# Transfers given out two at a time and a new order of work in a fused normalisation, state-space convolution and feed-forward kernel

## The chip, the core and the metric

The kernel runs on one core of one Trainium2 chip. A core has a matrix engine (TensorE, PE in the profile; its weight loads are PEld), a vector engine (VectorE, DVE), a scalar engine (ScalarE, ACT), a general engine (GpSimd, POOL), a sync engine (SyncE, SP) that here only gives out transfers, and 16 DMA engines that carry them. Data is worked on in SBUF, a memory of 128 partitions; PE writes its results into PSUM banks. Each engine runs its own list of instructions strictly in order and waits on semaphores for the others. The metric is device time in microseconds, the median of the timed runs.

## The reference

The input is one sequence of 2048 rows of 512 features. A condition vector gives six modulation vectors. The first half is a normalisation, a long convolution with a kernel built from 128 complex exponentials per feature, and a gated addition; the second half is a normalisation, a feed-forward part with squared ReLU, and a gated addition.

```python
def ssm(u, A_re, A_im, B_re, B_im, C_re, C_im, log_dt, Dskip):
    dt = jnp.exp(log_dt)[:, None]
    logdA = dt * (A_re + 1j * A_im)
    P = jnp.exp(logdA[:, :, None] * jnp.arange(L)[None, None, :])
    K = jnp.einsum("dn,dnl,dn->dl", Cc, P, dt * Bc).real
    # y = causal convolution of u with K along the sequence, through an FFT of length 2L
    return y + u * Dskip

def ffn(x, w1, b1, w2, b2):
    h = jnp.einsum("bsd,df->bsf", x, w1) + b1
    r = jnp.where(h > 0, h, 0)
    return jnp.einsum("bsf,fd->bsd", r * r, w2) + b2

sa, ca, ga, sb, cb, gb = split(silu(c) @ w_mod)
x = x + ga * ssm(layernorm(x) * (1 + ca) + sa, ...)
x = x + gb * ffn(layernorm(x) * (1 + cb) + sb, ...)
```

## The kernel before

The first half. The 2048 rows come in as 16 blocks of 128 rows by 512 features (`xt`, into tiles named `xy`). DVE takes their statistics (`bn_stats`, L595, L596), POOL makes the reciprocal deviation, and for every block `row_pieces` subtracts the mean and multiplies by the modulation (DVE, L657), scales a selection matrix (ACT, L659), multiplies by it on PE, which also adds the shift (L661, L664), and copies the result to the tile `big` (ACT, L667). PE has three banks named `ps` for this and for what follows, and one named `kg`.

The parameters of the convolution are worked out in two groups of four chunks of 64 features (`parameters`, L511 to L577): eight products on POOL (L526 to L533), roundings and absolute values on ACT (L535 to L545), an arctangent and a sine on ACT (L552, L561), shifts on DVE and integer additions on POOL (L564 to L574). `kgen_exp` fills tables with exponentials on ACT (L786).

The convolution runs on eight chunks of 64 features as a transform in two stages on PE, with constants that are loaded: `stage1` (L701, copied by ACT in L703) and `stage2` (L711, copied in L735). The input's spectrum goes through `u_pieces`; the kernel's 32 units are generated by POOL, ACT and DVE (`kgen_...`, L795 to L832), summed by PE into `kg` (L839) and transformed by `finish`. Products of the two spectra are taken on DVE (L849), which needs the input's spectrum twice: as it is, and with its two halves of 64 partitions exchanged. `swap_piece` makes the exchanged copy with two transfers from SBUF to SBUF, one for each half. PE sums the products (L857), DVE copies them (L863), and an inverse transform (L1024, with the constant `i2c`) gives the rows back.

The second half splits w1, w2 and the activations into a high and a low part of a faster number format (L973, L974, L977, L996) and computes 56 steps of two matmul groups (L1115 to L1118 and L1149 to L1151), three products each.

The order of the work. The program is first recorded in the order of the code; `ORDER` says, for each of the 32 kernel units, which pieces of the other work are recorded after it (r a row block, A to H an input chunk, 0 to 7 a swap, a to h a product chunk, x a table of exponentials, l the late modulation, w a load of a part of w1). Then `keep_order` puts every engine's instructions into one fixed list: it walks through the program with estimated durations, and at each step gives an engine, of the work that is ready, the one with the longest path to the end. `HURRY` adds or takes off urgency, in nanoseconds, for some kinds of work. The walk also has a model of how PE's instructions are fetched in packets, behind transfers. SP's list keeps the order of the recorded program. All loads, swaps and stores that matter here are given out by SP, one after the other: parameters and rows (L447 to L466), constants and modulation weights, swaps (L742), w1 (L933), `i2c` (L965), rows again for the gated addition (L984, L1040), w2 (L1084), stores (L1159). The list `behind` of pairs that `keep_order` takes is empty before.

Of the kernel before, what the change touches and what calls it, by code (L numbers as in the profile page):

```python
# [44 lines left out]
ORDER = (  # L45
    "rrrrrrrrrrrrrrrrCABCBCBlCBCBACBBA.AA.CAABA.xx.0Caaaa.a.aD1aa..bDbbbEE.DD.bDD2bEb.b.cDDEcccc.cxcc"
    "F3..EF.EEdddd.FFEd.GF4Fd.d.deGeeFeG.GGFx.HH.G.5HeeeeffGffGfww.6H..Hff.fH.gHHgggw.g.w7.hwghwhghgw"
    "w"
).split(".")
# [56 lines left out]


def weight(ins):

    out = ins.outs[0] if ins.outs and hasattr(ins.outs[0], "bass_ap") else None  # L110
    n = free_size(out) if out is not None else 1
    if "DMA" in type(ins).__name__:
        inside = not any("Dram" in type(a.bass_ap.tensor).__name__.title() for a in (*ins.ins, *ins.outs))
        return 60, n * out.ap[0][1] * 4 / (180 if inside else 360)
    match str(ins.engine).split(".")[-1]:
# [16 lines left out]
            if n == 1:  # L132
                t = 200
# [17 lines left out]
            t = 30  # L151
# [12 lines left out]
def keep_order(tc, traced, slots, in_turn, whole, urgent, behind):  # L164
# [107 lines left out]
    for _ in groups:  # L272
# [7 lines left out]
        if e == "PE":  # L280
# [55 lines left out]
def tile_adaln_ssm_ffn(  # L336
# [244 lines left out]

    urgent, behind = {}, []

# [154 lines left out]
    def swap_piece(c):  # L738
        xs, sw = xus[c], spectrum()
        sws[c] = sw  # L740
        for h in range(2):
            nc.sync.dma_start(sw[64 * h : 64 * h + 64], xs[64 - 64 * h : 128 - 64 * h])  # L742
        yield
# [184 lines left out]
    def load_pieces():  # L928
        for f, n in W1_PARTS:
            h = f // 896  # L930
            if f == 896 * h:
                raw1.append(held(kp, f"k0{h}", f"raw1{h}", [P, 4, 896]))
            nc.sync.dma_start(raw1[h][:, :, f - 896 * h : f - 896 * h + n], w1v[:, :, f : f + n])  # L933
            yield
# [29 lines left out]
    nc.gpsimd.tensor_copy(i2c[:, 0, 0, 0:1], runs(sws[NC - 1])[:, 0:1])  # L964
    nc.sync.dma_start(i2c, c_i2.rearrange("p (j r a) -> p j r a", j=64, r=2))  # L965

# [16 lines left out]
    for s in range(8):  # L983
        nc.sync.dma_start(xts[s], xt[s])  # L984
    w1la = held(ka, slots[na], "w1la", [P, 4, 512], FR)
# [30 lines left out]
    def inverse(s0, n):  # L1016
# [19 lines left out]
        for s in range(s0, s0 + n):  # L1036
            if s > 3:
                nc.gpsimd.tensor_add(x2[:, s], x2[:, s], d4(xts[s]))
                if s + 4 < 16:
                    nc.sync.dma_start(xts[s + 4], xt[s + 4])  # L1040

# [38 lines left out]
    def w2_split(t, n):  # L1080
        for i in range(n):
            wst = wsts[len(w2s) % 2]
            hi_, lo_ = t[:, 1024 * i : 1024 * i + 512], t[:, 1024 * i + 512 : 1024 * i + 1024]
            nc.sync.dma_start(wst, w2v[:, len(w2s)])  # L1084
            split(hi_, lo_, wst)
# [161 lines left out]
```

## Time and profile before

| | |
|---|---|
| runs | 639.13 us median of 3 (637.85 to 642.98) |
| the profiled execution | 637.81 us; span from the first to the last instruction 636.0 us |
| mean granted clock of PE | 0.99 |
| the first half | about 0 to 310 us |
| the steps of the feed-forward part | about 310 to 636 us |

A row of the profile names line, engine, operation, output and input tile and count; what stands in brackets is the time that the engine stood idle just before, and what ended it. "issue" there is a wait that nothing in the profile explains but the engine's own instruction supply. The page's slices show the course of the run: each digit is the busy share in a fortieth of the span, in tenths.

```profile
PE   1697897999999999898989999999999999999995
...
ACT  5957899889987948362856432253323433222220
POOL 6499699999999987039958100010000100000000
...
DMA  8942014022132403662333000100001000010001
```

### The profile page before, as it was taken

The numbers are of one execution on the slowest core, as the hardware profiler recorded it, in microseconds if no ns is written. First come the engines' busy times: TensorE is split into PE (matmuls) and PEld (weight loads), VectorE is DVE, ScalarE is ACT, GpSimd is POOL, SyncE is SP. The second block draws the span as 40 slices with busy tenths as digits, with TensorE's granted clock in tenths as the row PEclk, the third lists the DMA queues.
The fourth block names the chain that finished last, engine by engine and source line by source line (L and its number), as shares of the span: only waits on it lengthen the run. The fifth ranks groups of instructions, "written<-read, shape, count | busy, mean of one in ns | idle before, by whom it ended". The sixth has DMA issues, their size and how long they took to land.

```text
span 636.0 us, 21183 instructions
## 1 busy us (share of the span) xinstructions
PE 590.5 (93%) x9474; PEld 510.4 (80%) x9474; DVE 371.0 (58%) x652; ACT 349.6 (55%) x651; POOL 297.4 (47%) x247
## 2 busy tenths in 40 slices
PE   1697897999999999898989999999999999999995
PEld 1476797999998899897868888888888888888884
DVE  6886978899799688546655332533325332252223
ACT  5957899889987948362856432253323433222220
POOL 6499699999999987039958100010000100000000
PEclk9999999999999999899999999999999999999999
DMA  8942014022132403662333000100001000010001
GB/s 319 392 140 68 3 35 105 19 55 45 29 70 69 120 4 86 185 250 88 95 110 99 1 1 0 67 0 2 0 1 66 1 1 0 1 66 1 0 1 66
DMA packets 21707, 42.33 MB, mean 67 GB/s; under 512 B 3696, under 2 KB 9200, under 8 KB 20336
## 3 DMA queue, kind: packets, MB, share of 16 engines
q1 hardware_dynamic: 21184, 40.84, 21.0%
q8 instruction: 74, 1.21, 0.8%
q10 hardware_dynamic: 432, 0.14, 0.1%
q14 instruction: 17, 0.14, 0.1%
HBM read 28.39 MB, written 4.19 MB: 51 GB/s over the span
## 4 chain that ended last, share of the span: by engine, by line
PE 72%; ACT 9%; POOL 7%; DVE 5%; issue 4%; DMA 2%; DVEq 0%; SPq 0%; ACTq 0%; POOLq 0%
PE tg L1149 8%; PE tg L1151 8%; PE tg L1150 8%; PE ps L711 7%; PE ps L1115 6%; PE ps L701 6%; PE ps L1116 6%; PE ps L1118 6%; PE ps L857 6%; PE kg L839 3%; PE kg L1115 2%; PE kg L1116 2%; PE kg L1118 2%; PE tg L1024 1%; ACT xy L703 1%
## 5 line engine op out<-in xcount | busy, mean ns | idle before, releaser
L1135 ACT ACTIVATE xy<-ps,b1c 128x512 f32<-128x512 f32 x42 | 29.0, 690 | 126.2 <-PE ps L1118 126.2
L1137 DVE SCALAR_TENSOR_TENSOR ps<-ps,b1c,xy 128x512 f32<-128x512 f32 x42 | 31.8, 758 | 111.1 <-ACT xy L1135 111.1
L1060 POOL TENSOR_TENSOR big<-big,lo 128x512 f32<-128x512 f32 x12 | 15.7, 1306 | 151.8 <-DVE xy L1057 151.8
L711 PE MATMUL ps<-xy,t_sb 128*64 128x64 f32 x2048 | 67.4, 223 | 3.7 <-issue 2.5
L711 PEld LDWEIGHTS ps<-xy,t_sb 128*64 128x64 f32 x2048 | 63.9, 138 | 6.3 <-issue 3.0
L857 PE MATMUL ps<-e_sb,xy 128*64 128x128 f32 (+2 forms) x1152 | 64.2, 270 | 1.9 <-ACT xy L703 1.0
L857 PEld LDWEIGHTS ps<-e_sb,xy 128*64 128x64 f32 x1152 | 59.9, 142 | 3.6 <-ACT xy L703 1.4
L819 POOL TENSOR_TENSOR rtl<-tables 128x1024 f32<-128x1024 f32 x22 | 43.4, 1972 | 0.1
L703 ACT COPY xy<-ps 128x512 f32<-128x512 f32 x64 | 37.0, 598 | 7.7 <-PE ps L701 7.4
L849 DVE TENSOR_TENSOR xy<-ps,xy 128x512 f32<-128x512 f32 x64 | 39.9, 682 | 1.3 <-PE ps L711 1.1
L1115 PE MATMUL ps<-h0h,w1h 128*128 128x512 f32 (+1 forms) x96 | 36.0, 381 | 0.0
L795 POOL TENSOR_TENSOR rtl<-lo,big 128x1024 int32<-128x1024 int32 x16 | 34.3, 2145 | 3.1 <-ACT tg L807 2.5
L701 PE MATMUL ps<-d_sb,big 128*64 128x128 f32 x512 | 32.7, 275 | 2.9 <-ACT big L667 1.4
L701 PE MATMUL ps<-d_sb,ksb 128*64 128x128 f32 x512 | 34.3, 279 | 0.5 <-ACT xy L703 0.4
L863 DVE COPY big<-ps 128x256 f32<-128x256 f32 (+1 forms) x66 | 24.2, 407 | 18.0 <-PE ps L857 17.8
L795 POOL TENSOR_TENSOR llph<-lo,big 128x1024 int32<-128x1024 int32 x16 | 34.5, 2159 | 0.2 <-ACT tg L807 0.2
L701 PEld LDWEIGHTS ps<-d_sb,big 128*64 128x64 f32 x512 | 28.1, 137 | 4.3 <-ACT big L667 1.7
L1115 PE MATMUL ps<-h,w1h 128*128 128x512 f32 x80 | 31.4, 393 | 0.0
L1135 ACT ACTIVATE xy<-kg,b1c 128x512 f32<-128x512 f32 x14 | 9.7, 690 | 39.5 <-PE kg L1118 39.5
L1137 DVE SCALAR_TENSOR_TENSOR kg<-kg,b1c,xy 128x512 f32<-128x512 f32 x14 | 10.6, 756 | 34.0 <-ACT xy L1135 34.0
L701 PEld LDWEIGHTS ps<-d_sb,ksb 128*64 128x64 f32 x512 | 28.8, 140 | 1.6 <-ACT xy L703 0.7
L839 PE MATMUL kg<-rtl 128*32 128x64 f32 x1408 | 25.5, 221 | 4.3 <-issue 3.1
(287 smaller groups left out, 1606.7 us busy)
## 6 DMA issues: line engine op xcount, KB each, us to landing
xy<-xt SPq DMA_DIRECT2D x32, 256.0 KB, 5.5
xy<-xy SPq DMA_DIRECT2D x16, 512.0 KB, 6.0
xy<-w_mod SPq DMA_DIRECT2D x6, 1024.0 KB, 9.2
out_dram<-xy SPq DMA_DIRECT2D x16, 256.0 KB, 2.1
xy<-w SPq DMA_DIRECT2D x14, 256.0 KB, 2.7
raw<-w SPq DMA_DIRECT2D x6, 512.0 KB, 5.3
t_sb<-c_t SPq DMA_DIRECT2D x1, 2048.0 KB, 10.9
i2c<-c_i SPq DMA_DIRECT2D x1, 2048.0 KB, 9.9
```

What stands on the lines that cost most here:

```text
L701: nc.tensor.matmul(ps[64 * r : 64 * r + 64, 128 * i : 128 * i + 128], src[:, i], d1_sb[:, r], start=True, stop=True)
L711: nc.tensor.matmul(ps[64 * r : 64 * r + 64, 64 * i : 64 * i + 64].rearrange("p (h q t) -> p q h t", h=2, t=2), t2_sb[:, 8 * g + i, r], src ...
L795: nc.gpsimd.tensor_tensor(ph.rearrange("p d r (a b) -> p (d r) a b", a=4), bc(low_phase[:, us].rearrange("p d r b -> p (d r) b"), 2, 4), b ...
L819: nc.gpsimd.tensor_mul(am[:, 0, :, 32:96].rearrange("p d (v x) -> p d v x", v=2), bc(et[:, 256 + 8 * d0 : 384 + 8 * d0].rearrange("p (y a) ...
L839: nc.tensor.matmul(kps[32 * q : 32 * q + 32, d, :], am[:, r, 4 * q + d, 64:96], am[:, r, 4 * q + d, 0:64], start=(r == 0), stop=(r == 1))
L857: nc.tensor.matmul(ps[64 * m : 64 * m + 64], pairs(y)[:, g, i // 2, 64 * m : 64 * m + 64, i % 2], e1_sb[:, h].rearrange("p (r j) -> p r j" ...
L1115: pe.append(nc.tensor.matmul(ps, w1h[:, q, fs], hh[:, q, cols], start=(q == 0), stop=False))
L1116: pe.append(nc.tensor.matmul(ps, wl[:, q], hh[:, q, cols], start=False, stop=False))
L1118: pe.append(nc.tensor.matmul(ps, w1h[:, q, fs], hl[:, q, cols], start=False, stop=(q == 3)))
L1149: pe.append(nc.tensor.matmul(acc, r2l[:, ms], hi_, start=(t == 0), stop=False))
L1150: pe.append(nc.tensor.matmul(acc, r2h[:, ms], lo_, start=False, stop=False))
L1151: pe.append(nc.tensor.matmul(acc, r2h[:, ms], hi_, start=False, stop=(t == NF - 1)))
```

## The change

It has four parts. A helper `paced_load` issues a transfer on SP and, from the third one on, makes it wait until the transfer two places earlier in the same series has landed. The swaps, the loads of w1, `i2c`, the rows `xt` for the gated addition and w2 go through it; the first loads, the modulation weights and the stores don't. A swap's two halves are each cut in two along the free dimension, so that it is four transfers, and `i2c` is loaded in four pieces. The planner's constants for instruction packets and for the time that transfers occupy the queue are others. `ORDER` and `HURRY` are others.

```diff
+PACED = 2
-HURRY = (176674, 61960, 2605, 274089, 54201, -67055, -175605, 69371)
+HURRY = (147316, 134417, 27026, 378229, -185473, -185396, -357712, -713)
...
 ORDER = (
-    "rrrrrrrrrrrrrrrrCABCBCBlCBCBACBBA.AA.CAABA.xx.0Caaaa.a.aD1aa..bDbbbEE.DD.bDD2bEb.b.cDDEcccc.cxcc"
+    "rrrrrrrxrrxrrrrrrrCABCBCBCBCAACB.BBCBAAAAlAC...0aaaa1..aDaaa..DbbbbEE.D2D.DEbbD.xbDDb.EccccccE.F"
...
+    wait = mybir.DependencyInfo(mybir.DependencyClass.Sync, mybir.DependencyReason.DATA)
     for x, y in behind:
-        before[group[x]].add(group[y])
+        before[group[y.name]].add(group[x.name])
+        tc.add_manual_dep(y, x.name, wait, reason="pace")
...
-                    fetched = max(asked[0] + asked[1], min(behind_ns - 1800, asked[0] + 4300)) + 2350
-                asked = (max(t, fetched), 1100 if fetched > t else 600)
+                    fetched = max(asked[0] + asked[1], min(behind_ns, asked[0] + 4500)) + 2400
+                asked = (max(t, fetched), 1100 if fetched > t else 750)
...
-            queued.append((now, landed))
+            queued.append((now, landed + (-1000 if within(groups[g][0]) else -300)))
...
+    def paced_load(to, of):
+        ins = nc.sync.dma_start(to, of).ins
+        if len(paced) >= PACED:
+            behind.append((paced[-PACED], ins))
+        paced.append(ins)
...
         for h in range(2):
-            nc.sync.dma_start(sw[64 * h : 64 * h + 64], xs[64 - 64 * h : 128 - 64 * h])
+            for o in range(0, 2048, 1024):
+                paced_load(
+                    runs(sw)[64 * h : 64 * h + 64, o : o + 1024], runs(xs)[64 - 64 * h : 128 - 64 * h, o : o + 1024])
...
-    nc.sync.dma_start(i2c, c_i2.rearrange("p (j r a) -> p j r a", j=64, r=2))
+    for j in range(0, 64, 16):
+        paced_load(i2c[:, j : j + 16], c_i2.rearrange("p (j r a) -> p j r a", j=64, r=2)[:, j : j + 16])
```

The lines after the change are some 6 to 16 higher than before; all paced transfers carry line 591. How the change moves instructions is shown at two places. The first is SP's list at the end of the first half. Before (`raw` is w1 as loaded, `xy<-xy` the last swap):

```order
L933 DMA raw_4458<-w 128x4x256 x2
L933 DMA raw_4458<-w 128x4x128
L933 DMA raw_4458<-w 128x4x256
L742 DMA xy_97<-xy_94 64x2048 x2
L984 DMA xy_96<-xt 128x512 x2
L965 DMA i2c<-c_i 128x4096
L984 DMA xy_95<-xt 128x512 x4
```

SP's list at the same place after the change:

```order
L591 DMA raw_4391<-w 128x4x256 x2
L591 DMA xy_97<-xy_95 64x1024 x4
L591 DMA raw_4391<-w 128x4x128
L591 DMA raw_4391<-w 128x4x256
L591 DMA i2c<-c_i 128x1024 x4
L591 DMA xy_93<-xt 128x512 x4
```

The swap, now of four transfers, stands ahead of the last two loads of w1, and `i2c`, now of four, ahead of all rows `xt`.

The second place is the passage of the 16 row blocks, on DVE and on ACT. DVE's list before, at the third group of four blocks (`xy_91` holds the first four blocks, `xy_93` the third four, `xy_94` the last four; `st` and `mv` are statistics):

```order
L595 BN_STATS st_72<-xy_93 128x6
L595 BN_STATS st_73<-xy_93 128x6
L657 SCALAR_TENSOR_TENSOR xy_91<-xy_91,mv_71,kg_362 128x512 x3
L640 TENSOR_TENSOR s_360<-ps_157,gs_358 128x128
L595 BN_STATS st_74<-xy_93 128x6
L595 BN_STATS st_75<-xy_93 128x6
```

DVE's list after the change, where the first subtraction (now L670) stands:

```order
L575 TENSOR_SCALAR big_83<-big_83 128x4x64
L608 BN_STATS st_74<-xy_94 128x6
L608 BN_STATS st_75<-xy_94 128x6
L609 BN_AGGR mv_71<-st_73 128x2
L609 BN_AGGR mv_71<-st_74 128x2
L609 BN_AGGR mv_71<-st_75 128x2
L531 SCALAR_TENSOR_TENSOR big_83<-big_83 128x4x64
L670 SCALAR_TENSOR_TENSOR xy_91<-xy_91,mv_71,kg_362 128x512 x3
```

The first three subtractions moved from between the statistics of the third four blocks to behind those of the last four and behind the shifts of the first parameter group.

ACT's list before, from the fifth copy of a row block on (`big_84` takes the copied blocks, `big_83` holds the parameters, `ident` makes the selection matrix):

```order
L667 COPY big_84<-ps_159 128x128x4
L659 ACTIVATE big_83<-ident,mv_71 128x2x64
L667 COPY big_84<-ps_157 128x128x4
L659 ACTIVATE big_83<-ident,mv_71 128x2x64
L667 COPY big_84<-ps_158 128x128x4
```

ACT's list after the change, from the fifth copy on:

```order
L680 COPY big_84<-ps_159 128x128x4
L672 ACTIVATE big_83<-ident,mv_71 128x2x64
L541 ACTIVATE big_83<-big_83,magic 128x4x64
L542 ACTIVATE big_83<-big_83,magic 128x4x64
L550 ACTIVATE big_83<-big_83 128x4x64
L551 ACTIVATE big_83<-big_83 128x4x64
L543 ACTIVATE big_83<-big_83,unmagic 128x4x64
L680 COPY big_84<-ps_157 128x128x4
```

Five operations of the second parameter group (L535 to L545 before, L541 to L551 now) moved in ahead of the sixth copy; before, they stood behind the thirteenth and the fourteenth.

More of the change, by code (lines that the diff above doesn't have):

```diff
@@ L42 @@
 ON_DVE = {}
-HURRY = (176674, 61960, 2605, 274089, 54201, -67055, -175605, 69371)
+PACED = 2
+HURRY = (147316, 134417, 27026, 378229, -185473, -185396, -357712, -713)
 EXPS = [(0, 1), (1, 1), (2, 2), (4, 2), (6, 2)]
 ORDER = (
-    "rrrrrrrrrrrrrrrrCABCBCBlCBCBACBBA.AA.CAABA.xx.0Caaaa.a.aD1aa..bDbbbEE.DD.bDD2bEb.b.cDDEcccc.cxcc"
-    "F3..EF.EEdddd.FFEd.GF4Fd.d.deGeeFeG.GGFx.HH.G.5HeeeeffGffGfww.6H..Hff.fH.gHHgggw.g.w7.hwghwhghgw"
-    "w"
+    "rrrrrrrxrrxrrrrrrrCABCBCBCBCAACB.BBCBAAAAlAC...0aaaa1..aDaaa..DbbbbEE.D2D.DEbbD.xbDDb.EccccccE.F"
+    ".EEc3c.F.dddd.EdddFF4.dGFF..eGGeeeF.xGG.GeFHHe5Ge..effffGHf.wHf..HH.6ffwwwHg.g.gH.gww7g.gwgwhhhh"
+    "g"
 ).split(".")
@@ L105, in function_table, with within @@
     return {"Exp": 1, "Sin": 2, "Arctan": 3, "Sqrt": 4}.get(str(getattr(ins, "func", "")).split(".")[-1])
+def within(ins):
+    return not any("Dram" in type(a.bass_ap.tensor).__name__.title() for a in (*ins.ins, *ins.outs))
 def weight(ins):
@@ L112, in weight @@
     if "DMA" in type(ins).__name__:
-        inside = not any("Dram" in type(a.bass_ap.tensor).__name__.title() for a in (*ins.ins, *ins.outs))
-        return 60, n * out.ap[0][1] * 4 / (180 if inside else 360)
+        return 60, n * out.ap[0][1] * 4 / (180 if within(ins) else 360)
     match str(ins.engine).split(".")[-1]:
@@ L580, in parameters @@
         yield
-    urgent, behind = {}, []
+    urgent, behind, paced = {}, [], []
+    def paced_load(to, of):
[3 more added lines that the diff above has]
+        paced.append(ins)
     def hurry(start, ns):
@@ L932, in load_pieces @@
                 raw1.append(held(kp, f"k0{h}", f"raw1{h}", [P, 4, 896]))
-            nc.sync.dma_start(raw1[h][:, :, f - 896 * h : f - 896 * h + n], w1v[:, :, f : f + n])
+            paced_load(raw1[h][:, :, f - 896 * h : f - 896 * h + n], w1v[:, :, f : f + n])
             yield
@@ L983, in tile_adaln_ssm_ffn @@
     for s in range(8):
-        nc.sync.dma_start(xts[s], xt[s])
+        paced_load(xts[s], xt[s])
     w1la = held(ka, slots[na], "w1la", [P, 4, 512], FR)
@@ L1039, in inverse @@
                 if s + 4 < 16:
-                    nc.sync.dma_start(xts[s + 4], xt[s + 4])
+                    paced_load(xts[s + 4], xt[s + 4])
     def statistics(s):
@@ L1083, in w2_split @@
             hi_, lo_ = t[:, 1024 * i : 1024 * i + 512], t[:, 1024 * i + 512 : 1024 * i + 1024]
-            nc.sync.dma_start(wst, w2v[:, len(w2s)])
+            paced_load(wst, w2v[:, len(w2s)])
             split(hi_, lo_, wst)
```

## The prediction

> **What bounds the kernel now.** I read the page's first part, then its slices, the windows, what PE waited for, and the timelines of the places where PE stood still. The first two rows give busy time by engine, share and instructions; the third is one long window (busy us and count of PE, PEld, DVE, ACT, POOL, then granted clock, DMA share, GB/s); the fourth is a window of the second half.
>
> ```profile
> span 636.0 us, 21183 instructions
> PE 590.5 (93%) x9474; PEld 510.4 (80%) x9474; DVE 371.0 (58%) x652; ACT 349.6 (55%) x651; POOL 297.4 (47%) x247
> ...
> 85.00:345.00 260.00, 246.80 (x6922) 227.89 (x6918) 199.71 (x361) 193.63 (x327) 216.66 (x156) 0.99 0.32 87
> ...
> 360.00:380.00 20.00, 20.00 (x91) 16.53 (x90) 7.47 (x11) 8.40 (x15) 1.62 (x2) 1.00 0.00 0
> ```
>
> PE is the bound. From about 330 us it computes the two matmuls of the feed-forward part without a gap, on an order that the change keeps; nothing can be won there. PE is idle for 636.0 - 590.5 = 45.5 us: 260.0 - 246.8 = 13.2 us of it between 85 and 345, most of the rest ahead of 85, where data is not there yet. So the change is worth what it does to PE's gaps and to PE's clock. What PE waited for (total us, times, longest):
>
> ```profile
> PE kg L839 <- issue: 3.1, 3, 2.3
> ...
> PE ps L711 <- issue: 2.5, 4, 1.4
> ...
> PE tg L1024 <- issue: 1.8, 2, 1.1
> ...
> PE ps L1064 <- issue: 1.4, 1, 1.4
> ```
>
> These four make 3.1 + 2.5 + 1.8 + 1.4 = 8.8 us in which no other engine held PE: it waited for its own instructions. The timelines show why, twice:
>
> ```profile
> 92.16 14.78 SPq L742 DMA_DIRECT2D xy<-xy  x4
> ...
> 96.37 1.85 PE L711 MATMUL ps<-xy,t_sb 128*64 128x64 f32 x56 [0.48 <-ACT xy L703]
> ...
> 99.66 1.39 PE L711 MATMUL ps<-xy,t_sb 128*64 128x64 f32 x40 [1.43 <-issue]
> ...
> 254.89 2.99 SPq L933 DMA_DIRECT2D raw<-w  x4
> ...
> 261.47 0.64 PE L839 MATMUL kg<-rtl 128*32 128x64 f32 x26
> ...
> 262.83 1.11 SPq L742 DMA_DIRECT2D xy<-xy  x2
> ...
> 264.39 0.92 PE L839 MATMUL kg<-rtl 128*32 128x64 f32 x38 [2.28 <-issue]
> ```
>
> A group of 64 matmuls that needs nothing new breaks after 26, once with four loads of weights in flight, and one of L711 breaks with a swap in flight. Queue 8 brings the instructions of PE (packets, MB, share of the engines):
>
> ```profile
> q8 instruction: 74, 1.21, 0.8%
> ```
>
> 74 packets for PE's 9474 matmuls and 9474 weight loads are 256 instructions each, 128 pairs: PE stops where a packet ends and the next has not come, because it queues behind large transfers. The gap of 2.28 us has a second price, the clock:
>
> ```profile
> 260.00:265.00 5.00, 2.72 (x117) 2.48 (x112) 3.40 (x6) 0.00 (x0) 0.00 (x0) 1.00 0.69 181
> 265.00:270.00 5.00, 5.00 (x89) 4.66 (x83) 0.51 (x3) 0.96 (x2) 0.00 (x0) 0.66 0.71 159
> ```
>
> In the window after the gap the granted clock is 0.66: a loss of 0.34 x 5 = 1.7 us. A third place, with the DMA rate just ahead of it, and a fourth, where little moves:
>
> ```profile
> 284.00:288.00 4.00, 4.00 (x133) 4.00 (x132) 0.94 (x4) 0.00 (x0) 4.00 (x3) 1.00 1.00 373
> ...
> 290.91 1.05 PE L1024 MATMUL tg<-big,i2c 32*32 32x128 f32 x63 [1.14 <-issue]
> ...
> 295.00:300.00 5.00, 3.62 (x148) 3.02 (x121) 4.34 (x15) 2.52 (x5) 5.00 (x4) 0.91 0.21 59
> ```
>
> The 1.14 us follow a full DMA; between 295 and 300 PE loses 1.38 us with the DMA at a fifth.
>
> **The change, part by part.** The program runs the same matmuls, tile by tile; only order and transfers differ.
>
> *Swaps in pieces, loads by twos.* A swap was two transfers of 512 KB given out together and is now four of 256 KB, of which the third waits for the first to land. The rows give transfers, size and us to landing:
>
> ```profile
> xy<-xy SPq DMA_DIRECT2D x16, 512.0 KB, 6.0
> ...
> xy<-w SPq DMA_DIRECT2D x14, 256.0 KB, 2.7
> raw<-w SPq DMA_DIRECT2D x6, 512.0 KB, 5.3
> ...
> i2c<-c_i SPq DMA_DIRECT2D x1, 2048.0 KB, 9.9
> ```
>
> A swap is bounded by 6.0 us (pieces run as one) and 2 x 6.0 = 12.0 us (each pair as slow as a whole swap). Two rounds at the 2.7 us of a 256 KB load would be 5.4 us, so I take 7.5, near the lower end and 1.5 us later than now. No row shows PE or DVE waiting for a swap; the cover is the time between the swap and its product (L849). In the last one the swap is issued at 262.83, POOL learns of its landing at 271.04, and the product starts 5 us later:
>
> ```profile
> 271.04 0.18 POOL L964 COPY i2c<-xy 128x1 f32<-128x1 f32 x1 [16.17 <-DMA xy<-xy]
> ...
> 275.63 0.37 SPq L965 DMA_DIRECT2D i2c<-c_i  x1
> ...
> 276.12 2.48 DVE L849 TENSOR_TENSOR xy<-ps,xy 128x512 f32<-128x512 f32 x4
> ...
> 288.70 1.07 PE L1024 MATMUL tg<-big,i2c 32*32 32x128 f32 x65
> ```
>
> So 1.5 us cost 0; if the cover were gone they would cost up to 6 us once. [...]
>
> SP gives out transfers in order, so a waiting one holds those behind it. The tightest place is the end of the first half (the order of SP in the section on the change): the last swap has moved ahead of two loads of w1, and i2c, the constant of the inverse transform, ahead of every xt. Before, two xt stood between and waited for PE (what held SP's transfers: total us, times, longest):
>
> ```profile
> SPq L984 <- PE ps L857: 11.6, 4, 10.4
> ```
>
> So i2c went out at 275.63, 4.6 us after POOL's 271.04; now at about 271. Its four pieces by twos are bounded by 9.9 us and 4 x 5.3 = 21.2 us; two rounds at 5.3 make 10.6, landing at about 282, ahead of the 288.70 at which PE first uses it. I cost it at 0; at the upper end it lands at 292, and PE waits 4 us. The loads of xt and w2 behind it wait for a buffer either way, and cost 0.
>
> *What the pacing saves.* At most two pieces stand ahead of a packet of instructions: 0.5 MB of a swap or 1 MB of i2c, where 1 to 2 MB stood. Of the 8.8 us three gaps are plainly behind transfers: 1.43 + 2.28 + 1.14 = 4.85 us. Bounds: 0, or 1 to 2 lost, if the wait only moves to other places; 8.8, if every gap goes. I take four fifths of the three gaps and of the 1.7 us of clock, 3.9 and 1.4 us: nearer to the three rows than to either end.
>
> *The order of the row blocks, 25 to 62 us.* Here the new order loses. Each of the 16 blocks goes through DVE (subtraction, L657), PE (L661, L664) and ACT (copy, L667), and PE's next stage (L701) needs all 16. By the rows in the section on the change, DVE's first subtraction now stands behind the statistics of the last blocks and behind a chain that waits for ACT's arctangent; and ACT, after its fifth copy, does five operations of the second parameter group, of which L550 reads what POOL's eight products leave (L526 to L533 before, L532 to L539 now). The rows of before, from the timelines and, for 65 to 70, the windows:
>
> ```profile
> 24.92 2.04 DVE L657 SCALAR_TENSOR_TENSOR xy<-xy,mv,kg 128x512 f32<-128x512 f32 x3
> ...
> 37.84 1.08 PE L664 MATMUL ps<-xy,big 128*32 128x128 f32 x32
> ...
> 39.28 1.08 PE L664 MATMUL ps<-xy,big 128*32 128x128 f32 x32
> ...
> 43.08 0.73 POOL L527 TENSOR_TENSOR big<-big 128x256 f32<-128x256 f32 x1
> ...
> 49.65 0.73 POOL L528 TENSOR_TENSOR big<-big 128x256 f32<-128x256 f32 x1
> ...
> 53.58 1.95 POOL L819 TENSOR_TENSOR rtl<-tables 128x1024 f32<-128x1024 f32 x1
> ...
> 56.81 6.33 PE L701 MATMUL ps<-d_sb,big 128*64 128x128 f32 x112 [1.43 <-ACT big L667]
> ...
> 65.00:70.00 5.00, 3.75 (x70) 2.75 (x66) 4.83 (x15) 3.33 (x7) 1.63 (x3) 1.00 0.01 3
> ...
> 72.92 1.12 PE L839 MATMUL kg<-rtl 128*32 128x64 f32 x64 [1.20 <-DVE rtl L832]
> ```
>
> The subtraction moves from 24.92 to behind about eight more statistics and that chain, near 33.5, which alone makes the first blocks 5 us late. POOL was free for its products at 43.08, with one done earlier; with that one still to do it is now free near 42.3. Five products took 53.58 - 49.65 = 3.93 us, eight take 6.3 and end at 48.6; ACT's sixth copy comes near 49.6. PE has three banks, so its ninth block starts there; eight blocks at 39.28 - 37.84 = 1.44 us and the last copy reach 61.7, where 56.81 stood: 4.9 us late. Part comes back, since the late modulation no longer stands in this stage: PE's idle 1.25 us of the window from 65 and its 1.20 us ahead of the first kernel block, 2.45 us. Net +2.4, between -1 and +5.
>
> *The rest of the order.* PE changes matmul shape about as often as before; its other waits from 85 to 345, 13.2 - 8.8 = 4.4 us, I leave as they are, 0, between -3 and +4.
>
> The profiled execution took 637.81 us (span 636.0), 1.3 below the median of the runs, 639.13. Sum: 637.8 + 2.4 - 3.9 - 1.4 = 634.9, given as **635**.
>
> **The rivals.** *All packets come in time.* The 8.8 us go with the 1.7 us of clock: 637.8 + 2.4 - 10.5 = 630. For it: only late packets explain a stop inside a group. Against: the gap at 295, where the DMA is at a fifth. *The change doesn't do what it says:* packets come as late as before, the row blocks' 2.4 us remain: 640. [...] *Slower, by the head:* the 4.9 us are not made up, because ACT and POOL have no slack where they would have to (columns as above):
>
> ```profile
> 105.00:110.00 5.00, 4.17 (x118) 3.91 (x120) 4.96 (x9) 5.00 (x24) 4.92 (x4) 1.00 1.00 211
> ```
>
> Then the whole kernel generation comes 4.9 us late, PE's gap of some 3 us near 47 costs the 1.7 us of clock that the one at 262 cost, and PE waits 1.7 us more when the generation restarts: 646. It decides from a delay of 7.7 us on (645.5 - 637.8). Against it: from 65 to 70 ACT works 3.33 us of 5 and POOL 1.63. *Pieces come late:* the last swap lands at the 12.0 of its bound and PE waits once, 1 to 6 us: 640.
>
> **How the numbers follow.** Forecast 0.36 (631 to 639); all packets 0.30 (626 to 632); no effect 0.16; slower by the head 0.14; late pieces 0.04. Of 639.13, 1% is 6.4 us, about what a measurement of this kernel can tell from no change: faster is below 632.7, slower above 645.5. Faster: 0.29 of the second case and a quarter of the first, 0.38. Slower: most of the fourth and a little of the third, 0.15. Same 0.47. The range, 626 to 645, leaves out the ends of the second and the fourth case.
>
> **What would show it.** Right: the waits for issue from 85 to 345 fall from 8.8 to about 5 us, none of 2 us is left, the clock from 260 to 275 stays at 1.00, and L701 starts near 62 instead of 56.81. Wrong: L701 starts at 57, then the loss of 2 us falls away; or issue waits as long as before, then the pacing did nothing; or PE waits for DVE's products while swaps are in flight, then the pieces are late.

## The result, and the profile after

| | median us | lowest to highest | profiled execution | its span |
|---|---|---|---|---|
| before, 15 runs | 640.38 | 637.49 to 643.65 | 637.81 | 636.0 |
| changed, 15 runs | 633.82 | 631.82 to 639.61 | 632.78 | 631.0 |

The ratio is 0.9911 with a 95% interval of 0.9887 to 0.9936, which on 640.38 us is a gain of 5.7 us; the two profiled executions are 5.0 us apart. Predicted were 635 us, which is 2.9 us below the profiled execution of before, and, as likeliest (0.47), a change within 1%. So the time lies close to the forecast, but the gain is about twice the forecast one; and with medians that are 6.6 us or 1.0% apart, the change within 1% came out at its edge.

The first view is the list of PE's waits between 85 and 345 us in the changed kernel (engine, tile and line of what waited, what ended the wait, us in total, times, longest). It is to be compared with the list of before, in which the waits for `issue` were 9.4 us (the 8.8 of the prediction and 0.6 on L701), with 2.28 us as the longest:

```profile
PE tg L1040 <- issue: 2.9, 4, 1.0
PE ps L872 <- ACT xy L716: 1.4, 1, 1.4
PE tg L1165 <- ACT big L1051: 1.0, 1, 1.0
PE ps L724 <- issue: 0.7, 1, 0.7
PE ps L714 <- DVE xy L864: 0.7, 1, 0.7
PE ps L1080 <- ACT xy L1071: 0.4, 1, 0.4
```

The waits for `issue` are down to 2.9 + 0.7 = 3.6 us, none over 1.0, and those for kernel generation (L839, now L854) and for the residual addition's transposes (L1064, now L1080) are gone. In a second profiled execution of the same kernel (changed_again) they are 3.2 us, none over 0.8, but 1.0 of them on L854. The windows of the changed kernel for the head, the stretch as a whole and the place of the clock's dip (length; busy us and instructions of PE, PEld, DVE, ACT, POOL; PE's clock; DMA share; GB/s):

```profile
0.00:25.00 25.00, 8.74 (x96) 7.22 (x100) 17.91 (x60) 15.59 (x74) 15.77 (x32) 1.00 0.95 343
25.00:85.00 60.00, 48.75 (x1130) 38.83 (x1123) 46.09 (x71) 44.77 (x92) 47.59 (x47) 0.97 0.30 101
85.00:345.00 260.00, 252.05 (x7016) 231.20 (x7013) 203.81 (x372) 197.71 (x335) 217.85 (x157) 1.00 0.34 88
...
265.00:270.00 5.00, 5.00 (x108) 4.91 (x99) 1.00 (x4) 4.64 (x7) 0.00 (x0) 1.00 0.86 183
```

PE's idle time from 85 to 345 us fell from 13.2 us to 260 - 252.05 = 7.95, that is by 5.3 us, and the clock at 265 to 270 is 1.00 where it was 0.66. From 345 to 600 us PE is busy for 255.00 of 255 us in both kernels. So the gain stands where the prediction looked for it. The head, ahead of 85 us, is the place where it looked for a loss. The timelines of the changed kernel there (start, us busy, engine, line; in brackets the idle time ahead and what ended it), PE and then ACT:

```profile
34.34 1.94 PE L677 MATMUL ps<-xy,big 128*32 128x128 f32 x32 [3.28 <-DVE xy L670]
...
49.62 0.50 PE L674 MATMUL ps<-shift,pick 128*128 128x512 f32 x1 [2.75 <-ACT big L680]
...
63.39 8.08 PE L714 MATMUL ps<-d_sb,big 128*64 128x128 f32 x144 [0.70 <-ACT big L680]
...
73.78 1.12 PE L854 MATMUL kg<-rtl 128*32 128x64 f32 x64
```

```profile
47.17 0.51 ACT L541 ACTIVATE big<-big,magic 128x256 f32<-128x256 f32 x1 [3.67 <-POOL big L538]
```

The first block's matmuls start at 34.34, the ninth block at 49.62, the transform stage at 63.39 instead of 56.81; but the first kernel block (L854) starts at 73.78, only 0.9 us after the 72.92 of before, and no longer waits.

A swap now is this row of the DMA issues (transfers, size of one, median us to landing):

```profile
xy<-xy SPq DMA_DIRECT2D x32, 256.0 KB, 3.3
```

### The profile page after: what moved, and what is told of

Its sections match the earlier page's. It is cut to its first block, busy times and chain, and to the rows that moved or that the text cites. A ratio compares the mean times of both kernels' runs of the same rounds, so it can differ in the third digit from the quotient of the medians.

```text
span 631.0 us, 21224 instructions
## 1 busy us (share of the span) xinstructions
PE 588.5 (93%) x9474; PEld 507.8 (80%) x9474; DVE 371.3 (59%) x652; ACT 348.4 (55%) x651; POOL 297.8 (47%) x247
## 4 chain that ended last, share of the span: by engine, by line
PE 70%; POOL 10%; ACT 8%; DMA 4%; DVE 4%; issue 3%; DVEq 0%; SPq 0%; POOLq 0%
PE tg L1165 8%; PE tg L1167 8%; PE tg L1166 8%; PE ps L1131 6%; PE ps L1132 6%; PE ps L1134 6%; PE ps L724 5%; PE ps L714 4%; PE ps L872 4%; PE kg L854 3%; PE kg L1131 2%; PE kg L1132 2%; PE kg L1134 2%; PE tg L1040 2%; ACT tables L801 2%
## 5 line engine op out<-in xcount | busy, mean ns | idle before, releaser
L872 PE MATMUL ps<-e_sb,xy 128*64 128x128 f32 (+2 forms) x1152 | 63.5, 265 | 1.6 <-ACT xy L716 1.4
L872 PEld LDWEIGHTS ps<-e_sb,xy 128*64 128x64 f32 x1152 | 58.6, 139 | 3.1 <-ACT xy L716 1.9
L716 ACT COPY xy<-ps 128x512 f32<-128x512 f32 x64 | 36.9, 588 | 13.3 <-PE ps L714 13.2
L845 DVE TENSOR_TENSOR rtl<-rtl,tg 128x1024 f32<-128x1024 f32 x22 | 26.6, 1211 | 1.2 <-POOL rtl L834 1.2
```

The lines of the kernel that those rows point to most:

```text
L872: nc.tensor.matmul(ps[64 * m : 64 * m + 64], pairs(y)[:, g, i // 2, 64 * m : 64 * m + 64, i % 2], e1_sb[:, h].rearrange("p (r j) -> p r j" ...
```

## The experiments

The order is made by a planner that also sees the transfers, so undoing a transfer would reorder everything. Therefore the lists of all engines were taken as the planner had made them, for before and for the changed kernel, and written into the kernel as tables that are replayed. With them only what is named differs:

```diff
-    for _ in groups:
-        first = {e: min(r) if e == "SP" else min(r, key=lambda g: at[g]) for e, r in ready.items() if r}
...
+    for e in LISTS:
...
+        turns = np.cumsum(np.frombuffer(zlib.decompress(base64.b85decode(LISTS[e])), np.int16))
+        ordered = [i for g in turns for i in steps[g]]
+        for x, y in zip(ordered, ordered[1:]):
+            tc.add_manual_dep(y, x.name, info, reason="order")
+        loads = [i for i in ordered if i.name in paced]
+        for x, y in zip(loads, loads[PACED:]):
+            tc.add_manual_dep(y, x.name, wait, reason="pace")
```

Line numbers of these kernels are some 100 lower than those of the changed one. "Issue waits" are all waits of PE for `issue` between 85 and 345 us, from one profile each. Two executions with the same transfers and the same order gave 3.6 and 3.2 us (the changed kernel) and 3.3 and 4.9 us (early_head), so a difference of less than some 1.6 us between two rows says nothing. In the traces DVE, ACT and POOL run the same operations on the same tiles, in the same order, in both kernels marked "old" as in before, and in those marked "new" as in the changed kernel.

| order | transfers | ratio to before | 95% | issue waits us |
|---|---|---|---|---|
| old | whole, free (the kernel before) | 1 | | 9.4 |
| old | pieces, by twos | 1.0051 | 1.0028 to 1.0073 | 2.0 |
| old | pieces by twos for swaps and W1 alone | 0.9916 | 0.9884 to 0.9948 | 4.8 |
| new | whole, free | 0.9975 | 0.9951 to 1.0000 | 8.4 |
| new | whole, by twos | 0.9979 | 0.9959 to 0.9999 | 7.0 |
| new | pieces, free | 0.9944 | 0.9926 to 0.9963 | 7.1 |
| new | pieces, by twos (the changed kernel) | 0.9911 | 0.9887 to 0.9936 | 3.6 |
| new | pieces, one at a time | 1.0449 | 1.0395 to 1.0503 | 1.8 |

### Waits taken away (no_wait)

```diff
-        for x, y in zip(loads, loads[PACED:]):
-            tc.add_manual_dep(y, x.name, wait, reason="pace")
```

> The changed kernel with the order on every engine frozen as it is, the same pieces, and only the waits between transfers taken away: each transfer is issued as soon as its data allow. Theory A (the waits are what lets PE's instruction packets through): PE's waits for issue between 85 and 345 us come back, from 3.6 us to 6-10 us, and the time is 636 to 641 us, a ratio of 0.994 to 1.000 to the kernel before. Rival B (the new order, searched with better fetch times, or the smaller pieces, does it, and the waits add nothing): issue waits stay under 4 us and the ratio stays at 0.989 to 0.994.

Median 636.16 us, ratio 0.9944. PE's waits, from the same list as above:

```profile
PE kg L749 <- issue: 3.6, 3, 1.7
PE tg L935 <- issue: 3.0, 4, 1.4
```

With 0.5 us on the inner transform these are 7.1 us, 3.5 more than with waits; the ratio is 0.0033, or 2.1 us, higher. Theory A by its numbers, though the two intervals (up to 0.9936, from 0.9926) just touch.

### The new order with whole transfers (new_order_whole)

```diff
-            for o in range(0, 2048, 1024):
-                paced_load(
...
+            nc.sync.dma_start(sw[64 * h : 64 * h + 64], xs[64 - 64 * h : 128 - 64 * h])
...
-    for j in range(0, 64, 16):
-        paced_load(i2c[:, j : j + 16], c_i2.rearrange("p (j r a) -> p j r a", j=64, r=2)[:, j : j + 16])
+    nc.sync.dma_start(i2c, c_i2.rearrange("p (j r a) -> p j r a", j=64, r=2))
```

> The changed kernel with its order on every engine frozen, and the transfers as before: halves of 512 KB swapped whole, the constant in one load, nothing waits for another transfer. Theory A (the order by itself gains nothing between 85 and 345 us and loses some us in the head): issue waits of 7 us or more and a ratio of 0.997 to 1.006. Rival B (the order by itself is the gain): issue waits under 4 us, ratio 0.989 to 0.994.

Median 638.42 us, ratio 0.9975, issue waits 8.4 us, the longest behind a whole swap:

```profile
101.81 0.43 PE L747 MATMUL kg<-llph 128*32 128x64 f32 x13 [2.39 <-issue]
```

Theory A: the order alone does not bring the packets earlier. It does not lose either, as the head let me expect: it gains 1.6 us, between 0 and 3.1. The transfers are then worth 0.9975 - 0.9911 = 0.0064, or 4.1 us, for 8.4 - 3.6 = 4.8 us of issue waits.

### Whole transfers with waits (new_order_whole_paced)

The edit is the one above, with the two lines of the waits kept.

> The changed kernel's order frozen, with waits but without pieces: halves of 512 KB swapped whole and the constant in one load, issued by twos as they land. Theory A (what counts is how much is queued ahead of an instruction packet: two halves of 512 KB are as much as four pieces, so the waits alone do little): issue waits between 85 and 345 us of 6 to 8 us, ratio 0.994 to 0.998. Rival B (that something waits is enough, since it leaves gaps between pairs): issue waits of 3 to 4 us, ratio 0.990 to 0.993, as with pieces.

Median 638.80 us, ratio 0.9979, issue waits 7.0 us. Theory A. In issue waits, waiting without pieces does as little as pieces without waiting: a swap as twice 512 KB or as four free pieces leaves about 7 us, and only pieces by twos leave 3.6. In time, waits alone gain nothing on the whole transfers, while pieces alone may have gained 2.0 us (0.9944 against 0.9975, intervals that overlap).

### One transfer at a time (paced_by_one)

```diff
-PACED = 2
+PACED = 1
```

> The changed kernel's order and pieces, but only one transfer of 256 KB in flight instead of two. Theory A (packets wait for what is queued ahead): the issue waits before 285 us fall to 0.3 us or less; swaps and loads take longer (each piece then pays its start and its end alone), so token loads or W1 land late and PE waits 2 to 8 us for them between 240 and 310 us; ratio 0.992 to 1.002. Rival B (transfers have slack enough): no such wait, ratio 0.987 to 0.991.

Median 669.0 us, ratio 1.0449. The issue waits fall further, to 1.8 us (1.2 of them before 285 us, where A had 0.3), but the time rises by 28.7 us, far beyond the 2 to 8 us of data waits that were expected. VectorE's rows show the late transfers, PE's row what follows, and the windows the clock:

```profile
281.39 3.08 DVE L762 TENSOR_TENSOR xy<-ps,xy 128x512 f32<-128x512 f32 x5 [5.23 <-DMA xy<-xy]
...
308.60 1.41 DVE L947 TENSOR_TENSOR big<-xy,tg 128x256 f32<-128x256 f32 x4 [10.34 <-DMA xy<-xt]
```

```profile
309.73 3.02 PE L938 MATMUL tg<-big,i2c 32*32 32x128 f32 x128 [9.22 <-DVE big L947]
```

```profile
305.00:310.00 5.00, 0.27 (x15) 0.23 (x16) 1.40 (x4) 0.00 (x0) 0.00 (x0) 0.50 0.32 92
310.00:315.00 5.00, 4.64 (x136) 3.48 (x120) 3.45 (x14) 2.10 (x4) 2.03 (x2) 0.50 0.28 94
```

The last swap and the token loads are late by 5 and 10 us, PE stands, and its clock is 0.50 behind the gap. As expected a swap takes longer: the four pieces of the last one go out over 9.11 us from 269.76 on, where by twos they went out over 4.77, though a piece lands 2.9 us after its issue (median) and by twos 3.3. The direction is theory A's, its size is far off. From 85 to 345 us PE's idle time is 260 - 230.74 = 29.3 us, 16 more than before, and its mean clock is 0.93 instead of 0.99, which is up to 0.06 x 260 = 16 us more.

### The old order with all transfers paced (old_order_paced)

The lists of before, the pieces and the waits of the change.

> The kernel before with its order on every engine frozen, and only its transfers changed: swaps and the constant load in pieces, issued by twos as they land. Theory A (pacing alone brings the packets in time, whatever the order): the issue waits between 85 and 345 us fall from 8.8 to 3-4 us, the clock's dip at 265-270 us goes, the late head of the new order is absent, and the ratio is 0.985 to 0.992, at or below the changed kernel's 0.991. Rival B (the gain lies in the searched order and needs it): issue waits of 7 us or more and a ratio of 0.996 to 1.002.

Median 643.06 us, ratio 1.0051: slower. Neither theory: the issue waits fell to 2.0 us, below A's 3 to 4, and yet the time rose as in B. VectorE's and PE's timelines and two windows of this run:

```profile
295.33 1.42 DVE L948 TENSOR_TENSOR big<-xy,tg 128x256 f32<-128x256 f32 x4 [9.09 <-DMA xy<-xt]
```

```profile
296.47 3.02 PE L939 MATMUL tg<-big,i2c 32*32 32x128 f32 x128 [3.24 <-DVE big L948]
```

```profile
295.00:300.00 5.00, 3.02 (x128) 2.28 (x128) 3.38 (x11) 1.47 (x4) 1.26 (x2) 0.56 0.35 110
300.00:305.00 5.00, 4.22 (x38) 3.67 (x39) 4.40 (x15) 2.43 (x5) 5.00 (x5) 0.50 0.19 52
```

The rows of tokens for the first residual addition land late. In this order six of the eight stand right behind the inverse constant, and with all of them going by twos VectorE waits 9.09 us, PE 3.24, and the clock of the next ten microseconds is 0.56 and 0.50. In the changed kernel the same addition waits 1.03 us, and PE does not.

### The old order with only swaps and W1 paced (old_order_swaps)

```diff
-    for j in range(0, 64, 16):
-        paced_load(i2c[:, j : j + 16], c_i2.rearrange("p (j r a) -> p j r a", j=64, r=2)[:, j : j + 16])
+    nc.sync.dma_start(i2c, c_i2.rearrange("p (j r a) -> p j r a", j=64, r=2))
...
-        paced_load(xts[s], xt[s])
+        nc.sync.dma_start(xts[s], xt[s])
...
-            paced_load(wst, w2v[:, len(w2s)])
+            nc.sync.dma_start(wst, w2v[:, len(w2s)])
```

> The kernel before with its order frozen; only the swaps (in pieces) and the loads of W1 are issued by twos as they land, up to 270 us; the inverse constant comes in one load, and it, the token loads and the W2 loads wait for no other transfer, as before. Theory A (with all transfers paced, the old order lost because the token loads of the first residual additions landed late: VectorE waited 9.1 us for them): that wait is gone or under 3 us, the issue waits up to 275 us fall from 6.2 to under 2 us, those around 290-325 us (3.2) stay, and the ratio is 0.990 to 0.996. Rival B (pacing the swaps itself costs the old order something, late pieces that the products wait for): the ratio stays at 1.000 to 1.006.

Median 636.21 us, ratio 0.9916. VectorE waits for no transfer between 85 and 345 us any more, and the issue waits up to 275 us are 0.16 + 0.43 + 0.65 + 0.32 = 1.6 us, where before had 6.2. Two of the four rows:

```profile
235.98 0.39 PE L623 MATMUL ps<-xy,t_sb 128*64 128x64 f32 x6 [0.65 <-issue]
...
266.45 0.64 PE L753 MATMUL kg<-rtl 128*32 128x64 f32 x25 [0.32 <-issue]
```

Theory A. It is the plainest result of the study, though it rests on four runs: with the order of before kept on every engine, cutting up the swaps and pacing them and the loads of W1 gains 5.4 us (3.3 to 7.4), as much as the whole change.

### The head: both moves (early_head)

VectorE's first three subtractions go right behind the modulation's third product; ScalarE's five operations of the second group go behind the 10th copy, two sine tables behind the 13th, two square roots behind the 16th. In the tables of the lists (`d` is VectorE's, `a` ScalarE's):

```diff
-d
+d[:64] + d[79:82] + d[67:73] + d[64:67] + d[73:79] + d[82:]
-a
+a[:35] + a[40:48] + a[50:51] + a[35:40] + a[51:57] + a[48:50] + a[58:59] + a[60:62] + a[57:58] + a[59:60] + a[62:]
```

> The changed kernel with two moves in the head alone: DVE's first three row-block subtractions stand right behind the modulation's third product instead of behind the statistics of the last blocks and the range reduction; ACT's five operations of the second parameter group stand behind the 10th copy instead of the 5th (two sine tables behind the 13th, two square roots behind the 16th). Theory A (the head's 6.6 us of delay at the start of the transform stage still cost something): that stage starts at 56 to 59 us instead of 63.4, the first kernel block at 70 to 72 instead of 73.8, and the time falls 2 to 4 us below the changed kernel, a ratio of 0.985 to 0.989. Rival B (the second parameter group's chain sets the first kernel block anyway, and the delay was hidden): the stage starts earlier, the kernel block stays at 73 to 75, the ratio is 0.990 to 0.993.

Median 632.17 us of six runs, ratio 0.9891 (0.9862 to 0.9919). The stage starts at 56.94, the first kernel block at 69.97, 3.8 us earlier than in the changed kernel, but the time is only 1 to 2 us lower. The times of the head are A's, the ratio lies between the two.

### The head: VectorE's move alone (early_subtractions)

> The changed kernel with only VectorE's part of the early head: the first three row-block subtractions moved up, ScalarE's order left alone. Theory A (the prediction's: the ninth block starts only when ScalarE has done five operations that wait for GpSimd's products, whatever the first blocks do): first block near 31.5 instead of 34.3, ninth block still at 49 to 50 us, transform stage still at 61.5 to 63.5, ratio as the changed kernel's, 0.989 to 0.993. Rival B (the subtractions set the pace): the stage starts 2 to 3 us earlier and the time falls by 1 to 3 us.

Median 637.17 us, ratio 0.9949 (0.9925 to 0.9972). The subtractions do not set the pace, as A had it (the stage starts at 64.12, later than A's 61.5 to 63.5), but the ratio is worse than A's: some 2 us above the changed kernel, with intervals that overlap. PE's timeline and the windows:

```profile
50.17 0.79 PE L572 MATMUL ps<-shift,pick 128*128 128x512 f32 x1 [4.97 <-ACT big L578]
```

```profile
45.00:50.00 5.00, 0.20 (x8) 0.00 (x0) 2.86 (x6) 2.28 (x6) 4.61 (x7) 0.72 0.00 0
50.00:55.00 5.00, 4.83 (x67) 3.13 (x67) 4.93 (x4) 4.04 (x10) 4.76 (x5) 0.60 0.00 0
```

The early start only lengthens the gap ahead of the ninth block, from 2.75 to 4.97 us, and the clock drops in both windows, where the changed kernel has 1.00 and 0.66. But this trace also has a dip of the clock near 300 us, in two windows in which the changed kernel's first trace has 1.00:

```profile
295.00:300.00 5.00, 4.21 (x127) 2.98 (x126) 4.72 (x15) 3.22 (x8) 2.63 (x4) 0.63 0.49 156
300.00:305.00 5.00, 4.31 (x127) 2.91 (x128) 2.39 (x8) 2.69 (x5) 3.34 (x3) 0.50 0.39 115
```

So it is not shown that the 2 us are lost in the head.

### The head: ScalarE's move alone (early_copies)

> The changed kernel with only ScalarE's part of the early head: the five operations of the second group, two sine tables and two square roots moved behind later copies, VectorE's order left alone. Theory A (ScalarE's wait for GpSimd is what holds the ninth block): ninth block near 47 instead of 49.6, transform stage at 60 to 61.5 instead of 63.4, first kernel block at 71 to 73, ratio 0.987 to 0.991. Rival B (GpSimd's and VectorE's chain of the second group sets the first kernel block): stage earlier, kernel block at 73.5 or later, ratio 0.991 to 0.994.

Median 629.70 us, ratio 0.9861 (0.9825 to 0.9898), the fastest median of the study. PE's timeline and the windows:

```profile
59.72 2.84 PE L612 MATMUL ps<-d_sb,big 128*64 128x128 f32 x48 [0.70 <-ACT big L578]
...
70.97 1.12 PE L752 MATMUL kg<-rtl 128*32 128x64 f32 x64
```

```profile
45.00:50.00 5.00, 5.00 (x128) 3.68 (x131) 0.62 (x1) 3.21 (x8) 4.61 (x7) 1.00 0.02 3
50.00:55.00 5.00, 5.00 (x116) 3.29 (x104) 3.46 (x4) 4.47 (x12) 4.84 (x4) 1.00 0.02 3
```

The gap ahead of the ninth block is gone and the clock stays whole. Stage and kernel block start slightly earlier than A had them, and the ratio is just below A's 0.987 to 0.991: ScalarE's wait for GpSimd is what held the ninth block, and taking it away shortens the run.

### The changed kernel again, the early head again, and pacing only the swaps there

> The changed kernel itself, unaltered, beside the following three on one chip, since differences of a few tenths of a per cent are in question. Every theory expects 0.989 to 0.993. Theory A (the two groups of its times, 632-634 and 636-640 us, differ by a dip of PE's clock near 300 us, as the early subtractions' trace has it): if this trace has the dip, its time is 636 us or more; if not, 632 to 634. Rival B (the groups come from elsewhere): time and dip don't go together.

> The early head once more, to be compared with the changed kernel on the same chip; its first ratio, 0.989, had only six executions. Theory A (the late head costs the changed kernel 1 to 3 us): ratio 0.986 to 0.9895, and below the changed kernel's by 0.002 or more. Rival B (what the head gains is lost later to waits and the clock): ratios within 0.0015 of each other.

> The early head with pacing for the swaps and the loads of W1 alone; the inverse constant comes in one load, and it, the token loads and the W2 loads are free again. Theory A (pacing gains at the swaps and W1 loads, and is worth nothing after 270 us, where PE waits for packets with the DMA idle as well): issue waits up to 275 us under 2.5 us, those at 280-310 us 2 to 4 us, ratio 0.986 to 0.991, as the early head with all transfers paced. Rival B (the late pacing matters too): issue waits at 280-310 us of 5 us or more, ratio 0.992 to 0.996.

These three and the run above shared one chip. Changed again: 634.23 us, 0.9915 (0.9888 to 0.9942). Early head again: 632.35 us, 0.9905 (0.9871 to 0.9939), within 0.0015 of the changed kernel, as Rival B had it. With its first ratio of 0.9891 it lies between the changed kernel and ScalarE's move alone; what VectorE's move takes back is not settled. Early head with only swaps and W1 paced: 630.74 us, 0.9860 (0.9828 to 0.9892), issue waits up to 275 us 0.8 us, those of 280 to 310 us 4.1, a little above A's 2 to 4. It is Theory A: pacing after 270 us is worth nothing in the new order either, and may cost something (0.9860 without it, 0.9905 with it, intervals that overlap). On dips, the trace of the changed kernel again has one, though its execution took 634.9 us, less than theory A asked and more than its alternative allowed:

```profile
295.00:300.00 5.00, 4.26 (x189) 3.39 (x192) 4.45 (x16) 3.41 (x10) 2.55 (x2) 0.64 0.53 151
300.00:305.00 5.00, 4.66 (x95) 2.99 (x84) 2.77 (x6) 2.73 (x6) 2.54 (x2) 0.50 0.25 77
```

Time and dip go together in neither theory's way. Nor does the clock of the whole run divide the groups: it is 0.972 to 0.989 in the nine executions of the changed kernel above 636 us, and 0.976 to 0.998 in the seventeen below. Why the times fall into two groups stays open.

## Why the prediction was right, and where it was not

*Late packets as the cause: right, and now seen.* The trace shows the transfers of PE's instructions as queue q8. In before, PE stops for 2.28 us until 264.39. The queues from 261 to 262 us and from 262 to 263 (packets, MB, share of 16 engines):

```profile
q1 hardware_dynamic: 301, 0.29, 92.5%
q8 instruction: 1, 0.02, 7.2%
```

```profile
q1 hardware_dynamic: 24, 0.02, 6.5%
```

The packet moves as the loads of w1, given out from 254.89 on, drain, and PE goes on some 2.5 us later. On the new order, with only the transfers changed, the issue waits went 8.4, 7.1, 3.6 and 1.8 us (whole, pieces, pieces by twos, one at a time); the last of these is no clean comparison, since PE there also stands for data.

*Pacing saves 3.9 us and 1.4 us of clock: right in sum.* Predicted 5.3 us; measured 4.1 on the new order, and 5.4 (3.3 to 7.4) on the old one with only swaps and W1 paced. The issue waits fell by 5.8 us (9.4 to 3.6), 1.9 more than the term, since some of the waits under 1 us went as well. The 3.6 left are almost all on L1040. There PE runs through its instructions fast (112 matmuls in 1.76 us), and three stops of these last lines in other kernels had no transfer in the queues in the 3.5 us ahead of the half microsecond in which the packet moved (L1064 at 298.24 in before, the lines of L1040 at 301.62 in no_wait and 305.25 in new_order_whole). Ahead of stops of this kind there is nothing to pace: the rival "all packets in time" falls on them, as the prediction had it against the gap near 295. Of the four on L1040 in the changed kernel itself, the stop that ends at 297.87 is of the other kind: the DMA engines were full in the half microsecond before its packet (q1 at 100.8% from 295.00 to 295.55 us), with rows `xt`. In the half microsecond before the packets of the other three they were nearly empty (q1 at 8.0% at most).

*Pieces cost nothing: right for the changed kernel, though the swap of before was misread.* The row's 6.0 us is the median of one half, from its own issue to its own landing, and a swap is two halves. By the issues and landings in the traces the eight swaps took 6.7 to 8.0 us before, from the first issue to the last landing, and 7.5 to 8.5 us in pieces by twos. So the 7.5 us that the prediction took for a swap now are right, but a swap is only some 0.4 us later (medians 7.3 and 7.7), not 1.5. The prediction's own rows hint at it: the last swap was issued at 262.83, and POOL learned of it at 271.04. The traces show that a swap in pieces takes longer, by these 0.4 us, and the ratios (0.9911 by twos in pieces, 0.9979 by twos without) that here this costs less than the queue it clears. The inverse constant goes out from 274.83 on, not 271, lands at 286.0, not 282, and nobody waits for it. But the loads "behind it wait for a buffer either way, and cost 0" holds only in the new order: on the old one the token rows came 9.09 us late. So the rival of late pieces was real, though by twos it struck token loads and not swaps. With all transfers paced the old order gives 1.0051 and the new one 0.9911: what the new order is worth to the change is above all that it bears this pacing.

*The head, +2.4 us net: its path right, its size not settled.* The first subtraction was put near 33.5 and starts at 33.46; the ninth block 49.6, 49.62 seen; the stage 61.7, and 63.39 seen, 62.00 when the kernel ran again. Regained should be 2.45 us: between stage and first kernel block PE idled 0.82 + 0.36 + 0.65 + 1.20 = 3.03 us before and 0.36 now, which makes 2.7. (That the kernel block itself comes only 0.9 us late is no measure, since the late modulation's matmuls have moved behind it.) Up to 85 us PE's idle time is 25.6 us before, 85 - 8.74 - 48.75 = 27.5 in the changed kernel and 26.2 when it ran again; with what the clock took of 25 to 85 us, 60 us times its lack of 0.03, 0.03 and 0.09, the head costs +1.9 and +4.2 us. With whole transfers it is -0.3, since the clock happened to stay whole (1.00). These sums count too much clock: the second execution, whose clock was 0.51 and 0.50 from 30 to 40 us, began its ninth block at 49.62 like the first, after a gap of 1.43 us instead of 2.75, and reached the first kernel block 1.4 us earlier. There the clock that was lost ahead of the wait only shortened the wait. So the head's cost is known no better than about 0 to 4 us, and that 2.4 lies in the middle of this is no close hit.

*The rest of the order, put at 0 between -3 and +4: the step that failed.* The order as a whole was to cost 2.4 us and gained 1.6 (0 to 3.1) with whole transfers, 4.0 us off. With the head at the 2.4 of the sum, the rest is worth 4.0 us of gain, beyond its bound of 3. This is more than the whole difference between the gain of 2.9 us forecast and the 5.7 measured. That the time came out near 635 all the same is in part luck: the sum started from 637.8, and the runs of before that were measured with the change have a median of 640.4. The gain shows between 85 and 345 us, in the very stretch whose other waits the prediction left "as they are". The window of new_order_whole:

```profile
85.00:345.00 260.00, 248.75 (x6959) 228.91 (x6956) 200.35 (x370) 194.27 (x328) 214.87 (x154) 0.99 0.32 86
```

With whole transfers PE idles 260 - 248.75 = 11.25 us there instead of 13.2, 1.0 of the difference in waits for `issue` (8.4 against 9.4), and PE's clock loses 1.7 us instead of 3.4 (windows of 5 us below 1.00: 0.82 and 0.84 from 100 to 110, against 0.66, 0.91 and 0.75 at 265, 295 and 300). That is 3.6 us in one profile each, and rough: the profiled execution of new_order_whole is 3.0 us below that kernel's median. Which moves of the order bring it is not shown.

*The head as a cost that remains: right as a mechanism, its clock left out.* ScalarE's five operations behind the fifth copy were named as what holds the ninth block. Moving them away gained 0.9915 - 0.9861 = 0.0054, some 3.5 us (the intervals overlap a little, the medians are 4.5 us apart). PE's idle time up to 85 us is 85 - 59.55 = 25.45 us there instead of 27.5, and its clock from 25 to 85 us 1.00 instead of 0.97: the gap of 2.75 us and the clock of 0.66 behind it, from 50 to 55 us. This clock was in the rival "slower, by the head" and not in the sum.

*Packets as late as before, the rival at 640: wrong.* By count most packets came in time already in before: 11 stops for `issue` from 85 to 345 us stand against 74 packets of the whole run. But these 11 make 9.4 us, and a queue that is cut down is worth 4 to 5 us here.

## What to carry to other kernels

Where a matmul engine stops inside a group with nothing to wait for, look at what stands in the DMA queues two or three microseconds earlier: transfers that nobody waits for can hold its instructions (in before for 2.28 us until 264.39, behind loads of w1), and cutting the bytes in flight (here pieces and waits together, 3.6 us of stops instead of 9.4; on the new order waits alone gained nothing, 0.9979 against 0.9975) frees them. Pace only transfers that have slack: the same waits on loads that are needed next cost more than they gained (on the old order 1.0051, and 0.9916 where only swaps and W1 waited). And freeze the order when a transfer is tried, or a planner's new order hides what the transfer did.

## What the runs showed of the hardware

Twenty of the 33 stops for `issue` in four kernels (before, changed, no_wait, new_order_whole) were followed in half-microsecond windows: ahead of each, one packet of PE's instructions moved between 3.0 and 2.0 us before PE went on. The lag hardly depends on the load: the stop that ends at 301.62 in no_wait, with no transfer in the queues for six microseconds, shows it as well. At the 112 matmuls in 1.76 us that the changed kernel shows on L1040, the 128 pairs of a packet (9474 in 74) take an estimated 2.0 us, less than this lag. Whether this is why PE stops there with empty queues no run here shows.

Swaps with twice 512 KB in flight hold instructions up nearly as an unpaced queue does (7.0 us of issue waits against 8.4), with twice 256 KB about half as much (3.6 and 3.2 in two executions).

The clock of the head differs between executions of one kernel: 0.66 from 50 to 55 us in the first profile of the changed kernel, 1.00 there and 0.51 and 0.50 from 30 to 40 in the second, with the first kernel block at 73.78 and 72.40. So a single profile tells the head's times only to some 1.4 us.

The number format of the second half is the faster one in the trace of before: from 360 to 380 us PE takes 20.00 us for 91 matmuls, nearly all of 512 columns and in that format, about 0.22 us each, where eight of 128 columns in plain f32 (L503) took 2.05 us, about 0.26 us each, both at a clock of 1.00.
